# Tile 1 of a fused layer's start in two PSUM buffers, tile 2's statistics later, and other transfer prices in its list scheduler

## The chip, the cores and the metric

One core of one Trainium2 chip runs the whole kernel in one launch. The metric is the device time in microseconds (us), the median of three runs: 467.97 us (467.95 to 468.36) before the change. Beside it stands one profiled execution, of which every instruction is on record.

## The reference

The input x has 2048 rows of 512 numbers, all in float32. It is normalised row by row, goes through a windowed attention and through a two-layer block side by side, and the two results are multiplied:

```python
xn = _layernorm(x)                       # mean and variance over 512, eps 1e-5
qkv = xn @ wqkv                          # 512 x 1536; 32 heads of 16
# attention: position p sees p, p-2, ... p-14 (8 positions), softmax over those
s = attention(q, k, v) @ wo              # 512 x 512
h = relu(xn @ w1 + b1) ** 2              # 512 x 1792
g = silu(h @ w2 + b2)                    # 1792 x 512
out = x + s * g
```

## The kernel before

**Precision and tiles.** A float32 number is split into a high part (`high`, a ScalarE copy to the fast matmul type) and a low part (`low`, a subtraction on VectorE or on an engine that the scheduler chooses); `split` does both. A product of two split operands is three matmuls, high x high, high x low and low x high (`PASSES`, line 48). The rows of x come in 16 tiles of 128 rows. An even tile's split, transposed rows lie in `XA`; those of an odd tile lie half in `odd` and half in `XB`.

**Stages.** First the 16 tiles are normalised, transposed and multiplied with wqkv; the results go from the buffers `stg` to DRAM (`sq`, `sk`, `sv`). VectorE does the attention in eight units on data loaded from there, during most of the rest. Then TensorE does xn @ w1 (`ups`, in products called uX, uY and uZ), then h @ w2 (`down`, pb) mixed with the attention's output product (`out_product`, pw). From tile 4 on some products are made with seven multiplications in place of eight blocks, from sums of operands (`Sf`, `SA`, `SB`).

**Who sets the order.** Every instruction is recorded in a `Book`. A first pass, the draft, records the program; `arrange` (line 428) then plays it through up to 120 times with a list scheduler, `forward` (line 221), which holds a price for every instruction (`price`), a lag per engine (`LAGS`), and one wire for all transfers. It keeps the order whose end was earliest by those prices, and the second pass writes the instructions of each engine in that order. `tails` (line 365) gives each instruction its urgency with the same prices, and `landed` (line 390) adds waits of one DMA issue on an earlier transfer's landing where the plan has it so. TensorE's operations are chained as recorded (in `add`, line 154); the four other queues, SP's DMA issues among them, are the scheduler's to order. A DMA is priced in `add` at 600 ns of issue; in `forward` it takes the wire for its bytes divided by `RATE` (250 bytes per ns), no earlier than 800 ns after its issue, and has landed 1100 ns later.

**The start.** Up to `book.first = False` (line 1044) every queue keeps the order in which the code is written. There stand, for tiles 0 to 2 and the wqkv weights:

- `stats(t)` (line 821): two VectorE instructions for mean and variance (`st`, `mv`), one that adds the epsilon (`rs`), and the step on GpSimd that raises `rs` to the power -0.5 (the power step).
- `norm(t)`: one VectorE instruction that writes the normalised tile `early`; for tile 0 it is cut into two halves.
- `trans(t)` (line 880): four transposes on TensorE into one PSUM buffer `pxT` (`psT`, line 526, two buffers), then the `high` copies. Tile 0 uses both buffers.
- `keep_full(t)`: a ScalarE copy of the transposed tile to `fulls`; `lowx(t)`: the low parts.
- `qkv(t, s)` (line 972): the 12 matmuls of tile t with the q (s = 0), k (s = 1) or v (s = 2) weights, and the copy to `stg`. `late=True` does the products of the tile's high part first.
- The product of tile 0 with the k weights is done in plain float32 (eight instructions of TensorE, `pq<-wqraw,fulls`), with tile 1's transposes ahead of its last two.

The part that the change edits reads, from line 1014:

```python
    stats(1)
    low(*wq_parts(1, 0), V)
    ...
    norm(1)
    ...
    lows(0, 0)
    stats(2)
    qkv(1, 1, None, True)
    lows(0, 2)
    norm(2)
    stats(3)
    book.first = False
    constants()
    qkv(0, 0, lambda: highs(2, 0))
    trans(2)
```

Of the kernel before, what the change touches and what calls it, by code (L numbers as in the profile page):

```python
# [17 lines left out]
P = 128  # L18
# [40 lines left out]
WARM = 20  # L59
WARM2 = 1  # L60

RATE, AHEAD, ROUNDS, SPARE = 250.0, 2500.0, 120, 4000.0

LAGS = dict(P=250, V=160, A=170, G=150)

# [14 lines left out]
def elements(ap):  # L80
    n = 1
    for d in ap.shape[1:]:
        n *= d
    return n


class Book:
# [66 lines left out]
    def add(self, key, name, f, a, k):  # L154
        n = len(self.ops)
        engine = key
        if key == "E":
            engine = self.plan[1][n] if self.plan else "V"
            f = getattr(f[engine], name)
        ins = f(*a, **k)  # L160
        out = k["out"] if "out" in k else a[0]
        outs = [out] + ([k["accum_out"]] if "accum_out" in k else [])
        ins_ = [*(a if "out" in k else a[1:]), *(x for i, x in k.items() if i not in ("out", "accum_out"))]
        ins_ = [x for x in ins_ if isinstance(x, bass.AP)]
        two = sum(x.space != bass.MemoryType.PSUM and elements(x) > 1 for x in ins_) > (name != "tensor_scalar")
        if key == "E":
            op = Op(n, "E", ins, {e: self.price(e, name, k, ins_, out) for e in "VG"}, True)
        elif name == "dma_start":
            moved = 4
            for d in out.shape:  # L170
                moved *= d
            op = Op(n, "S", ins, 600, moved=moved)
        else:
            op = Op(n, engine, ins, self.price(engine, name, k, ins_, out),
                    engine == "V" and two or engine == "G" and elements(out) > 1 and name != "memset")
        op.early = self.first
        if self.first:
            if op.engine in self.heads:
                self.heads[op.engine].starts.append(op)
                op.waits += 1  # L180
            self.heads[op.engine] = op
        func = next((x for x in a if isinstance(x, mybir.ActivationFunctionType)), None)
        op.table = func if func in (AF.Exp, AF.Silu) else None
        op.stream = self.in_stream
        self.ops.append(op)
        if engine == "P":
            if "P" in self.last:
                self.edge(self.last["P"], op)
            self.last["P"] = op
        for x, writes in [(x, False) for x in ins_] + [(x, True) for x in outs]:  # L190
            r = self.region(x)
            if r is None:
                continue
            t, p0, p1, m = r
            writes = writes or t.space == "PSUM"
            if t not in op.tiles:
                op.tiles.append(t)
                if not t.users:
                    used = self.firsts.setdefault(t.slot, [])
                    if len(used) >= t.bufs:  # L200
                        t.behind = used[-1]
                    used.append(op)
                if t.behind not in (None, op):
                    t.behind.starts.append(op)
                    op.waits += 1
                t.users.append(op)
            kept = []
            for other, w, q0, q1, k_ in t.log:
                if (w or writes) and other is not op and p0 < q1 and q0 < p1 and m & k_:
                    self.edge(other, op)  # L210
                if not (writes and p0 <= q0 and q1 <= p1 and k_ & ~m == 0):
                    kept.append((other, w, q0, q1, k_))
            kept.append((op, writes, p0, p1, m))
            t.log = kept
        return ins
# [5 lines left out]
    def forward(self, urgency):  # L221
# [53 lines left out]
        while n:  # L275
# [57 lines left out]
                late = max(0.0, at - urgency[op.n])  # L333
            op.end = at + ns + LAGS.get(e, 0)
            if op.moved:
                wire = max(wire, at + ns + 800) + op.moved / RATE
                op.end = wire + 1100
            end = max(end, op.end)
            order.append(op)
            n -= 1  # L340
# [24 lines left out]
    def tails(self, order=None):  # L365

        extra, last = {}, None
        for op in self.ops:
            if op.stream and op.engine == "V":
                if last is not None:  # L370
                    extra[last.n] = op
                last = op
        follow = [list(op.after) + ([extra[op.n]] if op.n in extra else []) for op in self.ops]
        if order is None:
            order = self.ops
        else:
            for t in self.tiles.values():
                if t.prev is not None:
                    for op in t.prev.users:
                        follow[op.n] += t.users  # L380
        tail = [0.0] * len(self.ops)
        for op in reversed(order):
            ns = op.ns[op.given if order is not self.ops else "G"] if op.engine == "E" else op.ns
            cost = ns + (op.moved / RATE + 1900 if op.moved else LAGS.get(op.given, 150))
            tail[op.n] = max([cost + tail[b.n] if b.engine != op.engine or op.engine != "P" else ns + tail[b.n]
                              for b in follow[op.n]] or [cost])
        top = max(tail)
        return [top - t for t in tail]
# [117 lines left out]
def trace(ctx: ExitStack, tc: tile.TileContext, plan, x, wqkv, wo, w1, b1, w2, b2, out):  # L506
# [28 lines left out]
    def high(hi, lo, src):  # L535
        A.activation(hi, src, AF.Copy)

    def low(hi, lo, src, eng):
        eng.tensor_sub(lo, src, hi.bitcast(F32))
# [429 lines left out]
    def new_stg(t, s):  # L969
        stgs[s] = pstg.tile([P, GR, 2, CH], F32, name=f"stg{t}_{s}", tag="stg", bufs=3)  # L970

    def qkv(t, s, between=None, late=False, new=True):

        ps = psA(f"pq{t}_{s}")
        order = [(kt, a, b) for kt in range(KT) for a, b in PASSES]
        if late:
            order.sort(key=lambda o: o[1])
        for n, (kt, a, b) in enumerate(order):
            PE.matmul(ps, x_of(t, a, kt), wq[2 * s + kt // 2](b, kt % 2), start=n == 0, stop=n == 11,
                      skip_group_check=True)  # L980
            if between and n == 5:
                between()
        evacuate(t, s, ps, new)
# [28 lines left out]
        PE.transpose(pT[kt // 2][:, kt * P:(kt + 1) * P], xn[0][:, kt * P:(kt + 1) * P], ident)  # L1012
    idle(WARM2)
    stats(1)
    low(*wq_parts(1, 0), V)

    x0 = fulls[:, 0]
    for kt in (0, 2):
        cols = slice(kt * P, (kt + 2) * P)
        A.activation(x0[:, cols], pT[kt // 2][:, cols], AF.Copy)  # L1020
    norm(1)
    for kt in range(1, KT):
        split(*wq_parts(1, kt), V)
    for part in parts(0, x0):
        high(*part)
    ps = psA("pq0_1")
    for kt in range(KT):
        if kt == KT - 1:
            trans(1)
            keep_full(1, pTs[1])  # L1030
        PE.matmul(ps, x0[:, kt * P:(kt + 1) * P], raws[1, kt], start=kt == 0, stop=kt == KT - 1)
    lowx(1)
    for part in parts(0, x0):
        low(*part, V)
    evacuate(0, 1, ps)
    for kt in (0, 2):
        highs(0, kt)
    lows(0, 0)
    stats(2)
    qkv(1, 1, None, True)  # L1040
    lows(0, 2)
    norm(2)
    stats(3)
    book.first = False
    constants()
    qkv(0, 0, lambda: highs(2, 0))
    trans(2)
    keep_full(2, pTs[2])
    lows(2, 0)
# [512 lines left out]
```

## Time and profile before

| What | Value |
|---|---|
| Median of three runs | 467.97 us (467.95 to 468.36) |
| Profiled execution, its own time | 467.41 us |
| Its span, first to last instruction | 465.6 us (465.63) |
| TensorE busy | 459.5 us, 2037 matmuls and transposes |
| VectorE busy | 405.4 us |
| ScalarE busy | 302.5 us |
| GpSimd busy | 286.2 us |
| Bytes moved by DMA | 87.77 MB |

The times of the profile count from the span's start. Engines are named PE (TensorE's matmuls), PEld (its weight loads), DVE (VectorE), ACT (ScalarE), POOL (GpSimd) and SP (the queue that issues the DMAs). Almost every row carries line 160, since there the `Book` calls the engine; so rows are told apart by tile names, as out<-in. A row in order of time gives start, duration, engine, operation, tiles, shapes and count, and in brackets how long the engine sat idle before it and what ended that. Instructions of an engine that follow on each other are pipelined, so a row of several can overlap with the next.

### The profile page before, as it was taken

The page shows a single profiled execution, that of the slowest core. Times are in us where ns is not written, and L with a number is a line of the kernel's source. Part 1 is how long each engine was busy: PE and PEld are TensorE (multiplying, and loading weights), DVE is VectorE, ACT ScalarE, POOL GpSimd, SP SyncE. Part 2 cuts the span into 40 slices and gives each one's busy share as a digit, 9 for nine tenths or more (in the row PEclk, how much of TensorE's full clock was granted, in tenths as well). Part 3 has the DMA queues.
Part 4 walks back from the last instruction along what each step waited for, and adds up shares of the span by engine and source line. Part 5 has one row for each costly group of instructions (what it writes and reads, how often), then busy time and mean ns, then how long its engine had stood idle before and what let it go on. Part 6 is the DMA issues. An engine that isn't in the chain of part 4 may idle for free.

```text
span 465.6 us, 6191 instructions
## 1 busy us (share of the span) xinstructions
PE 459.5 (99%) x2037; PEld 378.7 (81%) x2037; DVE 405.4 (87%) x341; ACT 302.5 (65%) x569; POOL 286.2 (61%) x297
## 2 busy tenths in 40 slices
PE   8999999999999999999999999999999999999996
PEld 5788888888888888888888888888888888888885
DVE  5987996499999999999999979999999999589413
ACT  5756976974655748477684898687449544963331
POOL 2286343524999889975361699777656656465340
PEclk9999999999999999999999999999999999999999
DMA  8799789979989993962463395878853886260302
GB/s 277 220 237 280 246 226 280 264 169 277 261 227 263 242 289 126 242 176 69 107 184 75 119 236 176 207 226 259 207 139 101 230 199 204 92 178 25 113 1 91
DMA packets 71484, 87.77 MB, mean 188 GB/s; under 512 B 6684, under 2 KB 50972, under 8 KB 71452
## 3 DMA queue, kind: packets, MB, share of 16 engines
q1 hardware_dynamic: 71452, 87.38, 68.2%
q8 instruction: 16, 0.26, 0.2%
q14 instruction: 16, 0.13, 0.1%
HBM read 53.75 MB, written 30.47 MB: 181 GB/s over the span
## 4 chain that ended last, share of the span: by engine, by line
PE 97%; DVE 1%; DMA 1%; ACT 0%; issue 0%; POOL 0%
PE pb L160 33%; PE uX L160 16%; PE pq L160 13%; PE pm L160 12%; PE pw L160 9%; PE uZ L160 8%; PE uY L160 4%; DMA x<-in_A_x 1%; PE pxT L160 0%; DVE st L160 0%; DVE wq L160 0%; DVE z L160 0%; DVE wq0r L160 0%; DVE XA L160 0%; POOL rs L160 0%
## 5 line engine op out<-in xcount | busy, mean ns | idle before, releaser
L160 PE MATMUL pb<-w,h 128*128 128x512 f32 x592 | 149.1, 389 | 0.0
L160 PEld LDWEIGHTS pb<-w,h 128*128 128x128 f32 x592 | 110.9, 188 | 23.4 <-POOL h L160 0.4
L160 DVE TENSOR_TENSOR pr<-k,qp 128x2048 f32<-128x2048 f32 x32 | 72.8, 2274 | 6.5 <-ACT qp L160 4.8
L160 DVE TENSOR_TENSOR pv<-v,Lp 128x2048 f32<-128x2048 f32 x32 | 73.1, 2285 | 0.9
L160 DVE TENSOR_REDUCE v<-pv 128x256 f32<-128x2048 f32 x32 | 72.9, 2278 | 0.6
L160 DVE TENSOR_REDUCE L<-pr 128x128 f32<-128x2048 f32 x32 | 72.8, 2274 | 0.4
L160 POOL TENSOR_TENSOR h<-ut,h 128x512 fp32r<-128x512 f32 x25 | 32.2, 1299 | 37.4 <-ACT ut L160 30.9
L160 PE MATMUL pw<-wot,oT 128*128 128x512 f32 (+1 forms) x204 | 45.5, 376 | 0.0
L160 PEld LDWEIGHTS pw<-wot,oT 128*128 128x128 f32 x204 | 36.8, 188 | 7.1
L160 POOL TENSOR_TENSOR h<-u,h 128x256 fp32r<-128x256 f32 (+1 forms) x30 | 30.3, 1028 | 18.5 <-ACT u L160 14.8
L160 ACT ACTIVATE h<-ut 128x512 fp32r<-128x512 f32 x28 | 16.4, 626 | 27.5 <-PE pb L160 15.6
L160 PE MATMUL pq<-wq,XA 128*128 128x512 f32 x122 | 31.5, 391 | 0.3 <-DVE wq L160 0.3
L160 ACT ACTIVATE ut<-ut 128x512 f32<-128x512 f32 x42 | 24.9, 627 | 8.7 <-DMA ut<-su 6.4
L160 ACT ACTIVATE u<-uX,b1t 128x512 f32<-128x512 f32 x28 | 19.3, 688 | 17.2 <-PE uX L160 16.8
L160 DVE TENSOR_TENSOR z<-z,pw 128x512 f32<-128x512 f32 (+1 forms) x17 | 11.0, 648 | 20.9 <-ACT z L160 10.8
L160 POOL TENSOR_TENSOR oT<-oTf,oT 128x512 fp32r<-128x512 f32 x16 | 25.5, 1598 | 5.2 <-ACT oT L160 5.2
L160 POOL TENSOR_TENSOR u<-u,more 128x512 f32<-128x512 f32 x14 | 18.1, 1297 | 15.4 <-ACT more L160 15.0
L160 PEld LDWEIGHTS pq<-wq,XA 128*128 128x128 f32 x122 | 22.7, 188 | 5.3 <-DVE wq L160 0.7
L160 ACT ACTIVATE u<-u 128x512 f32<-128x512 f32 (+1 forms) x54 | 26.4, 528 | 0.4
L160 ACT ACTIVATE oT<-oTf 128x512 fp32r<-128x512 f32 x16 | 18.2, 1135 | 11.9 <-PE pw L160 10.2
L160 ACT ACTIVATE stg<-pm 128x512 f32<-128x512 f32 x30 | 17.9, 598 | 12.0 <-PE pm L160 10.3
L160 ACT ACTIVATE stg<-pq 128x512 f32<-128x512 f32 x24 | 14.4, 598 | 16.5 <-PE pq L160 13.6
(165 smaller groups left out, 1003.6 us busy)
## 6 DMA issues: line engine op xcount, KB each, us to landing
k<-sk SPq DMA_DIRECT2D x8, 960.0 KB, 7.5
v<-sv SPq DMA_DIRECT2D x8, 960.0 KB, 9.1
su<-u SPq DMA_DIRECT2D x28, 256.0 KB, 3.3
ut<-su SPq DMA_DIRECT2D x28, 256.0 KB, 3.6
x<-in_A_x SPq DMA_DIRECT2D x16, 256.0 KB, 4.2
sk<-stg SPq DMA_DIRECT2D x8, 512.0 KB, 4.9
sq<-stg SPq DMA_DIRECT2D x8, 512.0 KB, 4.4
sv<-stg SPq DMA_DIRECT2D x8, 512.0 KB, 4.1
```

The costliest lines, as they stand in the source:

```text
L160: ins = f(*a, **k)
```

## The change

It does four things. In the start, `low` of the first k weights moves from ahead of `norm(1)` to behind it. Tile 1 is transposed into two PSUM buffers, two transposes each; its high copies, its copies to `fulls` (now two) and its low parts each read one of them. The statistics of tile 2 (`stats(2)`) come behind the third `low` of the q weights in place of the second, the fourth follows them, and `qkv(0, 0)` does all products with the weights' high parts ahead of those with their low parts (`late` is now the place in the tuple by which the order is sorted: 1 the tile's part, 2 the weights'). And the list scheduler prices a transfer in a new way: 480 ns of issue, and a rate by the length of its contiguous pieces, the shorter of its two sides: 245 bytes per ns from 4096 bytes on, 340 from 2048, and 270 below.

```diff
-RATE, AHEAD, ROUNDS, SPARE = 250.0, 2500.0, 120, 4000.0
+AHEAD, ROUNDS, SPARE = 2500.0, 120, 4000.0
+
+ISSUE, BEFORE, BEHIND = 480, 800, 1100
+RATES = (4096, 245.0), (2048, 340.0), (0, 270.0)
...
+def contiguous(ap):
+    dims = list(ap.ap)
+    if ap.space != bass.MemoryType.DRAM:
+        dims = dims[1:]
+    run = 1
+    for step, count in sorted((d for d in dims if d[1] > 1), key=lambda d: d[0]):
+        if step != run:
+            break
+        run *= count
+    return 4 * run
...
-            op = Op(n, "S", ins, 600, moved=moved)
+            whole = min(contiguous(out), contiguous(k["in_"] if "in_" in k else a[1]))
+            op = Op(n, "S", ins, ISSUE, moved=moved / next(r for size, r in RATES if whole >= size))
...
-                wire = max(wire, at + ns + 800) + op.moved / RATE
-                op.end = wire + 1100
+                wire = max(wire, at + ns + BEFORE) + op.moved
+                op.end = wire + BEHIND
...
-            cost = ns + (op.moved / RATE + 1900 if op.moved else LAGS.get(op.given, 150))
+            cost = ns + (op.moved + 1900 if op.moved else LAGS.get(op.given, 150))
...
-    def qkv(t, s, between=None, late=False, new=True):
+    def qkv(t, s, between=None, late=0, new=True):
...
-            order.sort(key=lambda o: o[1])
+            order.sort(key=lambda o: o[late])
...
     stats(1)
-    low(*wq_parts(1, 0), V)
...
     norm(1)
+    low(*wq_parts(1, 0), V)
     for kt in range(1, KT):
         split(*wq_parts(1, kt), V)
     for part in parts(0, x0):
         high(*part)
+    second = []
     ps = psA("pq0_1")
     for kt in range(KT):
         if kt == KT - 1:
-            trans(1)
-            keep_full(1, pTs[1])
+            place(1)
+            pT = [psT(f"pxT1_{i}") for i in (0, 2)]
+            for i in range(KT):
+                PE.transpose(pT[i // 2][:, i * P:(i + 1) * P], xn[1][:, i * P:(i + 1) * P], ident)
+            for (hi, lo, _), t, cols in zip(parts(1, pT[0]), pT, (slice(0, 256), slice(256, 512))):
+                second.append((hi, lo, t[:, cols]))
+                high(*second[-1])
+            for i, t in enumerate(pT):
+                cols = slice(i * 256, i * 256 + 256)
+                A.activation(fulls[:, 1, cols], t[:, cols], AF.Copy)
         PE.matmul(ps, x0[:, kt * P:(kt + 1) * P], raws[1, kt], start=kt == 0, stop=kt == KT - 1)
-    lowx(1)
+    for part in second:
+        low(*part, V)
     for part in parts(0, x0):
         low(*part, V)
     evacuate(0, 1, ps)
     for kt in (0, 2):
         highs(0, kt)
     lows(0, 0)
+    low(*wq_parts(0, 2), V)
     stats(2)
-    qkv(1, 1, None, True)
-    lows(0, 2)
+    qkv(1, 1, None, 1)
+    low(*wq_parts(0, 3), V)
     norm(2)
     stats(3)
     book.first = False
     constants()
-    qkv(0, 0, lambda: highs(2, 0))
+    qkv(0, 0, lambda: highs(2, 0), 2)
     trans(2)
```

## Rows read from the trace of the kernel before

**Rows 1.** The page, part 1: busy time, share of the span, instructions.

```profile
PE 459.5 (99%) x2037; PEld 378.7 (81%) x2037; DVE 405.4 (87%) x341; ACT 302.5 (65%) x569; POOL 286.2 (61%) x297
```

**Rows 2.** The chain that ended last, in order of time: start, duration, what.

```profile
20.50 21.81 PE pq L160 x96
...
50.47 1.36 PE pq L160 x6
...
65.43 1.47 PE pq L160 x6
...
80.50 1.48 PE pq L160 x6
...
265.58 38.25 PE pb L160 x168
```

**Rows 3.** Instructions in order of time, TensorE's matmuls, 5 to 20.6 us.

```profile
5.78 0.76 PE L160 MATMUL pxT<-ident,early 128*128 128x128 f32 x4 [0.17 <-DVE early L160]
...
6.69 2.84 PE L160 MATMUL pq<-wqraw,fulls 128*128 128x512 f32 x6
...
14.55 0.61 PE L160 MATMUL pq<-wq,XA 128*128 128x512 f32 x2
15.43 1.44 PE L160 MATMUL pq<-wq,XA 128*128 128x512 f32 x5 [0.26 <-DVE wq L160]
16.71 0.60 PE L160 MATMUL pxT<-ident,early 128*128 128x128 f32 x4
...
19.90 0.60 PE L160 MATMUL pxT<-ident,early 128*128 128x128 f32 x4
```

**Rows 4.** The same view, VectorE, 3 to 20.6 us.

```profile
5.32 0.74 DVE L160 TENSOR_SCALAR early<-x,mv,rs 128x256 f32<-128x256 f32 x2 [0.68 <-POOL rs L160]
...
7.24 0.69 DVE L160 TENSOR_TENSOR wq<-wqraw,wq 128x512 fp32r<-128x512 f32 x1
8.38 0.55 DVE L160 TENSOR_SCALAR early<-x,mv,rs 128x512 f32<-128x512 f32 x1 [0.45 <-POOL rs L160]
8.84 1.89 DVE L160 TENSOR_TENSOR wq<-wqraw,wq 128x512 fp32r<-128x512 f32 x3
11.19 0.42 DVE L160 TENSOR_TENSOR odd<-pxT,odd 128x256 fp32r<-128x256 f32 x1 [0.46 <-ACT fulls L160]
...
13.67 0.69 DVE L160 BATCH_NORM_STATS2 st<-x 128x6 f32<-128x512 f32 x1
...
14.68 1.29 DVE L160 TENSOR_TENSOR wq<-wqraw,wq 128x512 fp32r<-128x512 f32 x2
15.89 0.54 DVE L160 TENSOR_SCALAR early<-x,mv,rs 128x512 f32<-128x512 f32 x1
...
18.97 0.55 DVE L160 TENSOR_SCALAR early<-x,mv,rs 128x512 f32<-128x512 f32 x1 [0.44 <-POOL rs L160]
```

**Rows 5.** The same view, GpSimd, 4 to 25 us: the power steps of tiles 0 to 2.

```profile
4.72 0.56 POOL L160 TENSOR_TENSOR rs<-rs,mhalf 128x1 f32<-128x1 f32 x1 [2.42 <-DVE rs L160]
7.38 0.96 POOL L160 TENSOR_TENSOR rs<-rs,mhalf 128x1 f32<-128x1 f32 x1 [2.11 <-DVE rs L160]
14.84 0.95 POOL L160 TENSOR_TENSOR rs<-rs,mhalf 128x1 f32<-128x1 f32 x1 [6.50 <-DVE rs L160]
```

**Rows 6.** The same view, ScalarE, 6 to 14 us: readers of the transposed tile 1.

```profile
10.01 0.39 ACT L160 ACTIVATE odd<-pxT 128x256 fp32r<-128x256 f32 x1 [0.42 <-PE pxT L160]
...
10.55 0.60 ACT L160 ACTIVATE fulls<-pxT 128x512 f32<-128x512 f32 x1
```

**Rows 7.** DMA issues (KB each, median us to landing), then two stretches (busy, PEclk, DMA).

```profile
x<-in_A_x SPq DMA_DIRECT2D x16, 256.0 KB, 4.2
...
w1r<-in_B_w SPq DMA_DIRECT2D x14, 256.0 KB, 4.7
...
8.00:14.00 6.00, 6.00 (x25) 4.09 (x24) 5.16 (x10) 5.56 (x12) 0.34 (x1) 1.00 1.05 395
20.50:42.00 21.50, 21.50 (x96) 17.74 (x96) 18.05 (x35) 11.61 (x24) 18.10 (x15) 1.00 0.99 251
```

## The prediction

> **What bounds the kernel now.** I read the page's busy times first: TensorE is busy for 99% of the span, VectorE for 87% [rows 1]. A busy TensorE need not be one at its peak, so the chain of waits in order of time comes next, for its pace. The reader is to see that it is a clock's pace: six matmuls of 128x512 take 1.36 us wherever nothing holds them up, so one takes 0.227 us, and 96 in a row from 20.50 us take 21.81 us, which is 0.03 us over 96 x 0.227. Where TensorE waits, the same six take longer: 1.47 at 65.43 (0.11 lost) and 1.48 at 80.50 (0.12 lost); and the 168 at 265.58 take 38.25 instead of 38.08 (0.17 lost) [rows 2]. So from 20.5 us to the last matmul the kernel loses about 0.4 us in all. The granted clock has nothing to give either: it is 1.00, the level of 2.4 GHz, in the stretch shown [rows 7].
>
> The start is the third view. From 14.55 to 16.71 us TensorE does seven matmuls; at 0.227 they are 1.59 us, so 0.57 us are lost, and the row at 15.43 names the subtraction that makes a low half of the q weights [rows 3]. Elsewhere between 6.69 and 20.5 us it runs through. The work ahead of 6.69 (first tile's load, statistics, transposes) is not touched by the change.
>
> Together 0.57 + 0.11 + 0.12 + 0.17 = 0.97 us. **That is the most that any order of the same matmuls can give back**, 0.21% of the time; 0.2%, 0.94 us, is about what a measurement of this kernel can tell from no change. The sum is made against the profiled execution, 467.41 us (span 465.63 and 1.78 around it); the median of the three runs is 0.56 above it, and I put the sum on the median.
>
> **Part 1: VectorE up to the second tile.** `low` of the first k weights moves behind `norm(1)`; in the whole start no DMA changes its place, and `qkv(1, 1)` keeps its order. Now it runs from 7.24 to 7.93 beside GpSimd's power step, which takes 0.96 us there and 0.56 for the first tile, where VectorE is idle [rows 4, 5]. Alone, the power step would end at 7.38 + 0.56 = 7.94 and `norm(1)` start at 7.98 instead of 8.38. TensorE gains nothing by it: its six float32 matmuls hold it until 9.53 whatever `norm(1)` does, and the second tile's transposes come behind them [rows 3]. Behind `norm(1)` (0.46 from its start to the next operation's) stand four `low` instead of three, 0.60 from start to start ((1.89 - 0.69)/2) [rows 4]: 7.98 + 0.46 + 4 x 0.60 = 10.84.
>
> **Part 2: two PSUM buffers.** Now VectorE waits 0.46 us, to 11.19, for ScalarE's copy of the whole transposed tile [rows 4]; ScalarE reads the tile from 10.01 to 11.16 [rows 6]. In two buffers each half has its own readers: ScalarE can begin two transposes (about 0.22 us) earlier, at 9.79, and does odd, XB, and two half copies at 0.27 from start to start ((10.55 - 10.01)/2), so the first half is free of ScalarE at about 9.79 + 2 x 0.27 + 0.39 = 10.72. VectorE, there at 10.84, finds it free. The copy in two parts costs ScalarE at most 2 x 0.39 - 0.60 = 0.18 us more, less than the 0.22 it starts earlier, so its four `high` of the q weights come no later than now and stay ahead of VectorE. The second tile's low halves thus start 0.35 us earlier, at 10.84 for 11.19. TensorE again gains nothing, it was not waiting for them.
>
> **Part 3: the third tile's statistics.** From 11.19 to the statistics at 13.67 VectorE spends 2.48 us [rows 4]; changed, that ends at 10.84 + 2.48 = 13.32. There one `low` of the q weights now stands first: 13.92. The statistics hold VectorE for 1.01 us (13.67 to 14.68), so the second `low` follows at 14.93 and ends at 15.62, where both had ended at 15.97. The 12 matmuls of `qkv(0, 0)`, now with all eight products of high weights first, start at 13.42 (five before the row at 14.55) and need the last low weight at 13.42 + 11 x 0.227 = 15.92: **the wait at 15.43 is gone**, and they are through at 16.14.
>
> **What is late next** is the third tile. Its transposes follow `qkv(0, 0)` on TensorE in any order of the draft, and need `norm(2)`, which needs the power step. That step starts 0.16 behind the `low` after the statistics (14.84 against 14.68), and beside a `low` it took 0.96 and 0.95 us [rows 4, 5]; so it runs from 15.09 to 16.04, `norm(2)` from 16.08 to 16.62 (0.54), and the transposes start at about 16.69: the first tile's start at 5.78, within 0.1 of the first half of its norm (5.32 and half of 0.74) [rows 3, 4]. Now they start at 16.71 [rows 3]. So the 0.57 us of waiting stays, as 0.55 between 16.14 and 16.69, and only its releaser changes. Queued behind the late `norm(2)` are the statistics and `norm(3)`, 0.19 us later (18.97 becomes 19.16) [rows 4]; its transposes come at 19.90 now [rows 3], and `norm(3)` would end at 19.71, so that cover still holds, with 0.13 to spare. Bounds for the start: from -0.57 (all of the wait goes) to +0.55 (the power step takes 0.96 only from 15.62 on: 16.58, norm to 17.16, transposes 17.23). I take the middle, -0.02, because both rows of the power step beside a `low` agree on 0.95.
>
> **Part 4: prices of transfers.** They cost nothing on the chip; they change the order in which the draft writes VectorE's, ScalarE's, GpSimd's and SP's instructions after the start. TensorE's order is as recorded, since the draft chains its operations. A load of x rows (256 KB, pieces of 2 KB) falls from 0.60 + 0.80 + 1.05 + 1.10 = 3.55 to 0.48 + 0.80 + 0.77 + 1.10 = 3.15 us; it took 4.2. A w1 load (512 B pieces) falls to 3.35; it took 4.7. So the latencies move away from these medians [rows 7], by up to 0.4 us, though the medians hold waiting in the queue, which the draft adds by itself. The rates move towards the trace: 395 GB/s came through in the first loads (2 KB pieces), 251 where the engines were full with mixed sizes [rows 7]. Below, the most to gain is the 0.40 us lost after 20.5; above, each transfer that a product is made to wait for just in time may come 0.4 us late. I take 0, as the old prices were also short of the medians and lost only 0.4 us in 445.
>
> **Sum:** 467.97 - 0.02 + 0 = 467.95 us.
>
> **Rivals.** *A, the third tile is in time.* If the power step isn't held up by the `low` issued at 14.93 it takes 0.56: it ends at 15.65, `norm(2)` at 16.23, transposes at 16.29, 0.42 earlier: 467.55. For it: the first row of [rows 5]. Against: the other two.
>
> *B, slower: transfers priced too cheap.* Place: loads that are needed just in time behind 20.5 us, where DMA is at a share of 0.99 [rows 7], so the turn, x and w1 loads and all that VectorE and GpSimd make of them. Price: 0.4 us for each load on which TensorE ends up waiting; it decides from the third such wait on (1.2 us). With four, 467.95 + 1.6 = 469.55. For it: both medians in [rows 7] stand above the new price, and VectorE, at 87%, has little room to catch up. Against: the same shortfall stood in the old draft at nearly as much, and only three waits of 0.1 to 0.2 us came of it [rows 2].
>
> *C, the power step is blocked outright.* In the trace it ends 0.41 us behind the `low` it runs beside (8.34 against 7.93) [rows 4, 5]. If it did all of its 0.56 behind it, it would end at 15.62 + 0.56 = 16.18 and the transposes come at 16.83: +0.12, 468.09. The Trainium skill, SBUF — State Buffer, section "Who interferes with whom", says so: a VectorE instruction with two SBUF inputs holds GpSimd's reads off until it is through. The trace agrees that it is held up, but not by the full length.
>
> *D, every wait goes*, also those after 20.5: 467.97 - 0.97 = 467.00.
>
> **How the numbers follow.** Forecast 0.57, A 0.15, B 0.14, C 0.10, D 0.04. Faster than 467.03 is D alone, 0.04; slower than 468.91 is B, 0.14; the rest, 0.82, is within 0.2%. The range reaches from 467.2, below A with some of the small waits gone, to 469.0, which takes in C and two waits at B's price (468.75); left out are D and B from three waits on, about 0.18.
>
> **What would show it.** Right: no idle time named by the low q weights around 15.4 us, but one named by `early` ahead of the transposes at about 16.7; the power step of tile 2 at 0.95 us from about 15.1; VectorE without the 0.46 us ahead of the second tile's low half; first product of tile 2 at about 17.05, as now. Wrong: transposes at 16.3 (A) or 16.8 (C), or, after 20.5 us, stretches of six matmuls above 1.36 us that add up to more than 1 us (B). The forecast is wrong as a whole if the time is more than 0.9 us from 467.95.

## The result, and the profile after

The changed kernel is **slower by 0.42%**: its median is 470.27 us over 16 runs (468.00 to 471.85), that of the kernel before 467.92 over 16 runs beside it (467.27 to 470.07), a ratio of 1.0042 with a 95% interval of 1.0027 to 1.0056 (this ratio goes with the means; the medians stand 0.50% apart). The forecast was 467.95, with 469.0 as the upper end: wrong, on the side of rival B.

The spread says more than the median. Of the 16 runs before, 14 lie between 467.27 and 468.36; the 16 after cover almost 4 us, and the shortest, 468.00, is near the time before. That shortest one is the profiled execution (span 466.2 us), so the rows below show the changed kernel when things went well. One run of `price_only` below, 515.23 us at a mean granted clock of 0.85, was a slow one and is left out of its numbers.

The page's busy times of the kernel after, against [rows 1]:

```profile
PE 460.1 (99%) x2037; PEld 379.8 (81%) x2037; DVE 403.0 (86%) x342; ACT 299.6 (64%) x568; POOL 282.2 (61%) x296
```

Nothing is to be seen in them. The start, in order of time: TensorE against [rows 3], VectorE against [rows 4], GpSimd against [rows 5]:

```profile
7.22 2.84 PE L175 MATMUL pq<-wqraw,fulls 128*128 128x512 f32 x6
...
16.21 0.61 PE L175 MATMUL pq<-wq,XA 128*128 128x512 f32 x2
17.21 0.63 PE L175 MATMUL pxT<-ident,early 128*128 128x128 f32 x4 [0.38 <-DVE early L175]
...
20.42 0.60 PE L175 MATMUL pxT<-ident,early 128*128 128x128 f32 x4
...
7.54 0.55 DVE L175 TENSOR_SCALAR early<-x,mv,rs 128x512 f32<-128x512 f32 x1 [0.67 <-POOL rs L175]
...
11.29 0.42 DVE L175 TENSOR_TENSOR odd<-pxT,odd 128x256 fp32r<-128x256 f32 x1 [0.80 <-ACT fulls L175]
...
15.39 0.68 DVE L175 TENSOR_TENSOR wq<-wqraw,wq 128x512 fp32r<-128x512 f32 x1
16.52 0.55 DVE L175 TENSOR_SCALAR early<-x,mv,rs 128x512 f32<-128x512 f32 x1 [0.44 <-POOL rs L175]
...
6.95 0.55 POOL L175 TENSOR_TENSOR rs<-rs,mhalf 128x1 f32<-128x1 f32 x1 [1.86 <-DVE rs L175]
15.56 0.93 POOL L175 TENSOR_TENSOR rs<-rs,mhalf 128x1 f32<-128x1 f32 x1 [8.05 <-DVE rs L175]
```

The wait for the low q weights is gone, and one named by `early` stands ahead of tile 2's transposes. From 16.21 two matmuls at 0.227 us end at 16.66, so that wait is 17.21 - 16.66 = 0.55 us. All of TensorE lies 0.53 us later than before here, since its first product starts at 7.22 for 6.69; that is not the change (last section). It accounts for most of the 0.59 between the two profiled executions, 468.00 and 467.41. Counted from the first product, tile 3's transposes come after 20.42 - 7.22 = 13.20 us, against 19.90 - 6.69 = 13.21 before: the edits of the start neither gain nor lose anything here, so what the changed kernel loses is lost behind the start.

Then the transfers: issues with median us to landing, then stretches of 10 us (PE, PEld, DVE, ACT, POOL busy, granted clock, DMA share, GB/s; a transfer counts in the stretch where it starts, so a share can pass 1), against [rows 7]:

```profile
x<-in_A_x SPq DMA_DIRECT2D x16, 256.0 KB, 5.6
...
w1r<-in_B_w SPq DMA_DIRECT2D x14, 256.0 KB, 5.3
...
20.50:42.00 21.50, 21.50 (x99) 17.84 (x98) 17.80 (x35) 13.02 (x26) 16.21 (x14) 1.00 1.03 271
50.00:60.00 10.00, 10.00 (x46) 8.15 (x45) 8.47 (x13) 8.24 (x20) 2.00 (x3) 1.00 1.07 267
60.00:70.00 10.00, 10.00 (x45) 8.10 (x45) 9.97 (x12) 9.80 (x24) 5.70 (x10) 1.00 1.04 300
70.00:80.00 10.00, 10.00 (x45) 8.28 (x45) 8.60 (x10) 9.18 (x24) 5.04 (x12) 1.00 1.02 254
```

The kernel before had, in the last three of these stretches:

```profile
50.00:60.00 10.00, 10.00 (x46) 8.29 (x45) 8.97 (x13) 9.98 (x24) 4.29 (x8) 1.00 0.70 228
60.00:70.00 10.00, 10.00 (x45) 8.09 (x45) 9.59 (x8) 6.53 (x14) 4.01 (x8) 1.00 0.84 218
70.00:80.00 10.00, 10.00 (x46) 8.29 (x45) 7.50 (x15) 5.97 (x12) 3.90 (x4) 1.00 1.05 267
```

The engines of the DMA had some room from 50 to 70 us before (0.70 and 0.84); after, there is none, and the same loads take longer to land, 5.6 us for 4.2 and 5.3 for 4.7. ScalarE is fuller too from 60 to 80 us: 9.80 and 9.18 us busy for 6.53 and 5.97. With the new prices the plan has transfers go out earlier: SP issues the x rows of tiles 14 and 15 at 64.52 and 65.07 us, for 77.47 and 77.87 before. The work that hangs on such transfers can come earlier with them.

**Where the lost time is** has to be read in a longer execution, not in the shortest. The changed kernel was run again, unaltered (`after_again`).

> The changed kernel once more, for a profile of one of its longer executions (its runs lay between 468.0 and 471.85 us; the first profile was of one of 468.0). Theory P: TensorE's waits behind 20.5 us add up to 1.5 to 3 us more than in the first profile, and follow a transfer's landing. Theory S: the extra time is lost ahead of 20.5 us, in the start or in the level of the clock there.

Median 468.86 over 12 runs (468.15 to 473.45), ratio 1.0037 (1.0016 to 1.0058): the loss and the spread are there again, though the median is 1.4 us below that of the first 16 runs. The profile is of an execution of 470.45 us. What TensorE waited for in it (total us, times, longest):

```profile
PE pq L175 <- ACT stg L175: 1.1, 1, 1.1
PE pxT L175 <- DVE early L175: 0.4, 1, 0.4
```

The second stands in that view of the shortest execution too; the first does not. Counted from start to start of TensorE's matmuls, with 0.227 us taken off each, the execution of 470.45 us loses 2.6 us behind 20.5 us and the shortest 0.3. Of the 2.6, 1.4 are lost at 82.4 us, where this wait is; the rest is in losses of 0.1 to 0.4 us each, the larger ones ahead of matmuls that read `SA` (60.0 us) and `h` (295.6 and 323.2 us). What led to those was not followed. The longest one can be followed back, instruction by instruction (in order of time, VectorE, ScalarE, TensorE, `after_again`):

```profile
74.06 1.32 DVE L175 STREAM_TRANSPOSE pxT<-turn 128x512 f32<-128x512 f32 x2 [1.33 <-DMA turn<-turn]
...
74.83 0.60 ACT L175 ACTIVATE XA<-pxT 128x512 fp32r<-128x512 f32 x1 [1.00 <-DVE pxT L175]
75.42 0.39 ACT L175 ACTIVATE odd<-pxT 128x256 fp32r<-128x256 f32 x1
...
81.27 0.60 ACT L175 ACTIVATE stg<-pm 128x512 f32<-128x512 f32 x1
81.74 0.61 ACT L175 ACTIVATE stg<-pq 128x512 f32<-128x512 f32 x1
...
82.40 0.97 PE L175 MATMUL pq<-wq,odd 128*128 128x512 f32 x3 [1.12 <-ACT stg L175]
```

and the same instructions in the shortest execution of the same kernel:

```profile
72.54 1.31 DVE L175 STREAM_TRANSPOSE pxT<-turn 128x512 f32<-128x512 f32 x2
...
73.53 0.59 ACT L175 ACTIVATE XA<-pxT 128x512 fp32r<-128x512 f32 x1
...
80.32 0.62 ACT L175 ACTIVATE stg<-pq 128x512 f32<-128x512 f32 x1
...
80.99 1.66 PE L175 MATMUL pq<-wq,odd 128*128 128x512 f32 x6
```

The four loads of turned tiles 10 and 11 (`turn`) were issued within 0.2 us of each other in the two (66.52 and 66.70), and the last landed at 72.41 in the one and 73.94 in the other. VectorE's transposes, ScalarE's copy `XA` and the ScalarE copy that empties the PSUM buffer (`stg<-pq`) follow 1.52, 1.30 and 1.42 us later. ScalarE has no gap from 74.83 to 83.05, so it hands on all of its delay, and TensorE starts 1.41 later. In the kernel before, ScalarE reached the same evacuation with three gaps behind its `XA` copy, 1.34 + 0.70 + 1.04 = 3.08 us; by an estimate that takes what ended these gaps as not hanging on the load, a late load could have eaten that much (ScalarE in order of time, before):

```profile
76.23 0.60 ACT L160 ACTIVATE Lp<-L 128x512 f32<-128x512 f32 x1 [1.34 <-POOL L L160]
77.53 0.60 ACT L160 ACTIVATE stg<-pm 128x512 f32<-128x512 f32 x1 [0.70 <-DMA sv<-stg]
79.18 0.60 ACT L160 ACTIVATE stg<-pm 128x512 f32<-128x512 f32 x1 [1.04 <-PE pm L160]
```

### The profile page after: what moved, and what is told of

Its sections match the earlier page's. It is cut to its first block, busy times and chain, and to the rows that moved or that the text cites. A ratio compares the mean times of both kernels' runs of the same rounds, so it can differ in the third digit from the quotient of the medians.

```text
span 466.2 us, 6205 instructions
## 1 busy us (share of the span) xinstructions
PE 460.1 (99%) x2037; PEld 379.8 (81%) x2037; DVE 403.0 (86%) x342; ACT 299.6 (64%) x568; POOL 282.2 (61%) x296
## 4 chain that ended last, share of the span: by engine, by line
PE 97%; DVE 1%; POOL 0%; issue 0%; ACT 0%; DVEq 0%; POOLq 0%
PE pb L175 33%; PE uX L175 16%; PE pq L175 13%; PE pm L175 12%; PE pw L175 9%; PE uZ L175 8%; PE uY L175 4%; PE warm L175 1%; PE pxT L175 0%; DVE wq L175 0%; POOL rs L175 0%; DVE z L175 0%; DVE wq0r L175 0%; DVE st L175 0%; DVE XA L175 0%
## 5 line engine op out<-in xcount | busy, mean ns | idle before, releaser
L175 POOL TENSOR_TENSOR h<-ut,h 128x512 fp32r<-128x512 f32 x23 | 29.6, 1294 | 40.7 <-ACT ut L175 36.3
L175 POOL TENSOR_TENSOR h<-u,h 128x256 fp32r<-128x256 f32 (+1 forms) x32 | 32.0, 1022 | 21.1 <-ACT u L175 20.0
```

## The experiments

**1. The two halves of the change, apart.** `start_only` is the changed kernel with the old prices, `price_only` the kernel before with the new ones.

```diff
 # start_only, against the kernel after
-AHEAD, ROUNDS, SPARE = 2500.0, 120, 4000.0
...
-ISSUE, BEFORE, BEHIND = 480, 800, 1100
-RATES = (4096, 245.0), (2048, 340.0), (0, 270.0)
+RATE, AHEAD, ROUNDS, SPARE = 250.0, 2500.0, 120, 4000.0
...
-            op = Op(n, "S", ins, ISSUE, moved=moved / next(r for size, r in RATES if whole >= size))
+            op = Op(n, "S", ins, 600, moved=moved)
...
```

> The edits of the start alone, with the old transfer prices. Theory P (the new prices make a plan in which transfers are needed just in time, and their varying landing turns into waits of TensorE): 467.9 us, within 0.2% of the kernel before, with its spread of about 1 us. Theory S (the start itself got worse): about 470 us, and the profile shows over 1.5 us more lost on TensorE ahead of 20.5 us than the kernel before. Theory R (any new order that the scheduler draws has its own tight places, whatever edit caused it): anything from 467 to 471 us, the loss in the profile lying behind 20.5 us.

> The new transfer prices alone, with the old start. Theory P: 469.5 to 470.5 us with a spread of 2 us or more, as the changed kernel, and the loss is behind 20.5 us. Theory S: 467.9 us. Theory R: anything from 467 to 471 us, and not the same waits as in the changed kernel.

`start_only`: 468.88 us (468.64 to 469.24, 9 runs), ratio 1.0024 (1.0015 to 1.0033). `price_only`: 470.19 us (469.51 to 470.28, 5 runs), ratio 1.0044 (1.0031 to 1.0057). So each half costs time alone, and the prices cost more than twice as much. No theory met both: P had said 467.9 for `start_only`, and for `price_only` a spread of 2 us or more. Neither has a wide spread (0.6 and 0.8 us), so the spread of the changed kernel is not brought about by the new prices as such.

The loss of `start_only` is in the start (TensorE, VectorE and GpSimd in order of time, `start_only`):

```profile
17.08 0.63 PE L160 MATMUL pxT<-ident,early 128*128 128x128 f32 x4 [0.58 <-DVE early L160]
...
19.46 1.50 DVE L160 TENSOR_SCALAR early<-x,mv,rs 128x512 f32<-128x512 f32 x1 [0.44 <-POOL rs L160]
...
19.40 1.28 POOL L160 TENSOR_TENSOR wq<-wqraw,wq 128x512 fp32r<-128x512 f32 x1
```

`norm(3)` takes 1.50 us in place of 0.55, beside a subtraction on GpSimd that began 0.06 us ahead of it, and tile 3's transposes come 0.82 us late; ahead of tile 2's, TensorE loses 0.85 us, for 0.55 in the kernel after. With the old prices the draft gives that subtraction to GpSimd at that point; with the new ones it does not (after, `norm(3)` takes 0.55 and nothing waits for it). So this cost belongs to a draft, not to the edits of the start as such.

The profile of `price_only` shows three waits of TensorE for `stg`, at 65.7, 81.6 and 97.9 us; the second is at the place of the wait of `after_again` (total us, times, longest):

```profile
PE pq L175 <- ACT stg L175: 2.0, 3, 1.1
```

That is its loss, but its own plan had waits of 1.28 us at 81.0, 0.58 at 96.6 and 0.30 at 111.9, 2.2 us in all, since the draft played by the new prices did not find a better order. So `price_only` does not tell a bad plan from a plan that is missed. The next runs do.

**2. The rates alone.** The changed kernel, with the old 600 ns for an issue.

```diff
-ISSUE, BEFORE, BEHIND = 480, 800, 1100
+ISSUE, BEFORE, BEHIND = 600, 800, 1100
```

> The changed kernel with the rates by length of pieces but the old 600 ns of issue. Theory T1 (the rates are what is too cheap): transfers behind 50 us land later than the plan has it, as in the changed kernel by 1 to 3 us, and runs spread over 2 us or more, median 469 to 470.5. Theory T2 (the issue price is what is too cheap): landings at or ahead of the plan, spread under 1 us, median 468 to 468.9.

470.79 us (470.19 to 471.59, 5 runs), ratio 1.0060 (1.0046 to 1.0073). Theory T2 is out, and T1 missed its figures: the median is above its band, and the spread is 1.4 us. This plan has no waits of its own behind the start and still loses 2.8 us. Behind 20.5 us the profiled execution, of 470.31 us, loses 2.3 us, ahead of matmuls that read the `SA` sums, at 74.2 (0.25) and 75.5 (0.34), and `h`, at 349.2 (0.34) and 393.5 (0.65), with about 0.1 behind each (what TensorE waited for, total us, times, longest, `rates_only`):

```profile
PE pb L175 <- POOL h L175: 0.7, 2, 0.5
PE pm L175 <- POOL SA L175: 0.2, 1, 0.2
```

The rates suffice for a loss; the price of an issue is not needed: `start_only`, which differs from this run in the rates alone, took 468.88 us. The waits are at other places than in `after_again`, so it is no single load that was misplaced. That these waits follow from a late landing is not shown.

**3. Plan against trace.** Each draft leaves a planned landing for each transfer, and the traces have the real ones. The table takes the transfers issued from 40 to 125 us and gives the median of real less planned landing; then how far TensorE itself stands behind its plan there, on average; the difference is how early (below 0) the data came for those who wait for it. The runs are the profiled executions.

```
                landing - plan   TensorE - plan   difference
before              -2.13           -0.4            -1.7
start_only          -0.31           +1.0            -1.3
stats_first         +0.22           +1.7            -1.5
price_only          +0.99           +0.9            +0.1
after               +1.03           +1.1            -0.1
after_again         +1.67           +1.9            -0.2
rates_only          +0.82           +1.3            -0.5
```

With the old prices the data came 1.3 to 1.7 us ahead of plan, with the new ones between 0.5 us ahead and on plan. Nobody had written a margin into the old prices; most of it goes with the flat rate of 250, for `start_only`, which has that rate, stands at -1.3 and `rates_only`, which differs from it in the rates alone, at -0.5. In the kernel before, 1.3 of its 1.7 us are there at the issue already: the transfers go out that much ahead of plan, by the same reckoning. On plan in the median means late for nearly half of the transfers, and in the kernel after a tenth of them came 1.1 us late or more.

**4. The x rows ahead of a late load, moved behind it.** The changed kernel's plan is kept, instruction by instruction, but SP issues the turned tiles 10 and 11 ahead of the x rows of tiles 14 and 15, which stood before them.

```diff
-        plan = trace(draft_tc, None, *copies)
-    trace(tc, plan, *aps)
+        order, given, landed = trace(draft_tc, None, *copies)
+    loads, rows = (545, 546), (541, 542, 543, 544)
+    order = [n for n in order if n not in loads]
+    at = max(order.index(n) for n in rows) + 1
+    order[at:at] = loads
+    landed = [(n, m) for n, m in landed if not (n in loads or n in rows and m in loads)]
+    trace(tc, (order, given, landed), *aps)
```

> The changed kernel with its own plan kept to the letter, but for one thing: the two loads of x rows (tiles 14 and 15, 512 KB) that SP issues just ahead of the four transfers that turn tiles 10 and 11 are issued just behind those. Theory T (a full DMA queue makes the turned tiles land late; VectorE's transposes of them wait, ScalarE's copies of those wait with the evacuations queued behind them, no PSUM buffer comes free, TensorE waits at about 81 us): the turned tiles land 1.5 to 2 us earlier, no execution waits at 81 us, the runs above 469.5 us become rare, median 468.3 to 468.9. Theory U (the executions differ for another reason, such as the clock or the end): same median and spread as the changed kernel, 468 to 473 us.

474.59 us (472.55 to 477.49, 6 runs), ratio 1.0146 (1.0114 to 1.0178): far slower, and the expectation missed. The turned tiles were issued no earlier: the first of the four went out at 66.52 us, as in the shortest execution of the kernel after (66.52) and 0.18 us before that of `after_again`, though two loads fewer stood ahead of it. The last of them landed at 72.15, for 72.41 and 73.94. But the plan lets the next issue, a load of k, wait for the landing of the x rows, so that it went out at 73.14 in place of 69.74, the store of `stg` behind it landed at 81.53 for 78.10, and the buffer was free that much later (ScalarE and TensorE in order of time, then windows with the granted clock as the third number from the end, `moved`):

```profile
81.61 0.60 ACT L175 ACTIVATE stg<-pm 128x512 f32<-128x512 f32 x1 [2.85 <-DMA sv<-stg]
...
84.67 2.93 PE L175 MATMUL pq<-wq,odd 128*128 128x512 f32 x6 [3.59 <-ACT stg L175]
...
84.00:85.00 1.00, 0.33 (x1) 0.33 (x2) 1.00 (x2) 0.98 (x2) 0.09 (x1) 0.50 1.03 269
...
90.00:91.00 1.00, 1.00 (x6) 0.83 (x5) 0.25 (x1) 0.88 (x2) 0.00 (x0) 1.00 1.09 129
```

The move was no test of the one load, since it came no earlier on SP. It does show the mechanism a second time, by another transfer: a landing, then ScalarE in order, then the PSUM buffer, then TensorE. And it shows how little slack is around: two issues exchanged with four cost 4 us and more. Part of that is the clock: behind the pause of 3.59 us TensorE ran at a granted clock of 0.50 (last section).

**5. The start, another way.** The start of the changed kernel at the old prices, but with the statistics of tile 2 ahead of both `low`.

```diff
-    low(*wq_parts(0, 2), V)
     stats(2)
     qkv(1, 1, None, 1)
-    low(*wq_parts(0, 3), V)
+    lows(0, 2)
```

> Old prices; of the start's edits all but the last: the third tile's statistics stay ahead of both remaining low parts of the q weights. By the theory of the start (the low part that is issued between the statistics and the norm holds the power step up, and the transposes of the third tile wait for it) the power step ends about 0.6 us earlier than with the start's edits alone, and the wait ahead of the third tile's transposes (0.85 us there) falls under 0.3 us, with at most 0.2 us come back ahead of the products with the low q weights. The rival (the wait follows from the two PSUM buffers and the later first low part) leaves it at 0.8 us. Time 468.0 to 468.6 against 468.9 of the start's edits alone, if the new plan has no waits of its own.

470.02 us (469.41 to 470.49, 5 runs), ratio 1.0043 (1.0029 to 1.0056): the expectation missed, with a wait of 1.00 us where under 0.3 was said. GpSimd, VectorE and TensorE in order of time, `stats_first`:

```profile
16.54 1.35 POOL L160 TENSOR_TENSOR wq<-wqraw,wq 128x512 fp32r<-128x512 f32 x1
...
16.68 1.49 DVE L160 TENSOR_SCALAR early<-x,mv,rs 128x512 f32<-128x512 f32 x1
...
18.32 0.63 PE L160 MATMUL pxT<-ident,early 128*128 128x128 f32 x4 [1.00 <-DVE early L160]
```

The draft put a subtraction of GpSimd beside `norm(2)` this time, with the price seen in `start_only`: 1.49 us for 0.55. The power step began at 15.62, no earlier than in the kernel after, as the draft had also slipped another VectorE instruction ahead of the statistics. So it says nothing of where the statistics are best placed; it repeats the blocked norm. Behind 23 us this execution has one wait, for `stg` at 127.7 us (0.5 us), and its own plan has one there too. With the old prices, then, neither `start_only` nor `stats_first` shows a wait behind 23 us that its plan lacks; the three plans drawn with the new prices all do (1.3 us at 82.4 in `after_again`, four of 0.25 to 0.65 in `rates_only`, 0.46 at 65.7 in `price_only`). The plan of the kernel before shows none in its own profile, and one of 0.3 us, at 321.5, in `late_frozen` (experiment 7). So three plans on each side speak against any new order having such tight places of its own (Theory R), but do not rule it out.

**6. Margin, tested directly.** If the margin in the plan is what counts, the same extra load must cost the kernel after, and not the kernel before. Both plans are kept as they are; on the chip the stores of two transposed tiles (6 and 7) write each row twice, 512 KB more, into a spare place of which half is read back. The output's computation is unchanged.

```diff
-        dma(sr[t], full)
+        if plan and t in (6, 7):
+            dma(wide[t - 6], full[:, None, :].to_broadcast([P, 2, D]))
+        else:
+            dma(sr[t], full)
...
-            dma(raw[t][i], sr[t][:, i * 256:(i + 1) * 256])
+            src = wide[t - 6][:, 0] if plan and t in (6, 7) else sr[t]
+            dma(raw[t][i], src[:, i * 256:(i + 1) * 256])
```

> The kernel before with its own plan, in which the two stores of transposed tiles 6 and 7 write twice the bytes (each row also into a spare place that nobody reads): 512 KB more, about 2 us of the DMA engines, at 53 to 67 us. Theory M (the old prices left transfers landing ahead of the plan by more than 1 us, and that margin hides a disturbance): the time stays within 0.5 us of the kernel before, and no wait over 0.5 us appears on TensorE between 55 and 125 us. Rival N (both plans are as tight, and the changed one only met worse luck): 1 to 2 us slower, with such a wait.

> The same added 512 KB in the changed kernel with its own plan, at about 63 us. Theory M (the new prices left no margin): 2 us or more slower than the changed kernel (470 us and more at the least, median 471.5 to 474), with a wait of 2 us or more on TensorE at 81 us behind evacuations of ScalarE. Rival N: slower by as much as the kernel before is with the same bytes.

`before_2x`: 467.94 us (467.26 to 468.42, 11 runs), ratio 0.9997 (0.9988 to 1.0005). `after_2x`: 470.88 us (469.83 to 471.33, 6 runs), ratio to the kernel before 1.0060 (1.0048 to 1.0072); its shortest run is 1.8 us above the shortest of the kernel after, its median a little under the band expected. Against the kernel after, which was not run beside it, the median is 0.6 us higher (first 16 runs) or 2.0 (`after_again`), and 15 of those 28 runs are shorter than its shortest; Theory M had said 2 us or more. TensorE at the critical place in `before_2x`:

```profile
80.18 1.64 PE L160 MATMUL pq<-wq,odd 128*128 128x512 f32 x6
```

and the chain in `after_2x` (VectorE, ScalarE, TensorE in order of time):

```profile
75.16 1.32 DVE L175 STREAM_TRANSPOSE pxT<-turn 128x512 f32<-128x512 f32 x2 [1.99 <-DMA turn<-turn]
...
82.83 0.60 ACT L175 ACTIVATE stg<-pq 128x512 f32<-128x512 f32 x1
...
83.48 1.65 PE L175 MATMUL pq<-wq,odd 128*128 128x512 f32 x6 [1.71 <-ACT stg L175]
```

The same bytes cost nothing in the old plan. In the new one the wait of `after_again` is 1.71 us for 1.12, by the same chain, 1.1 us later at each link; a wait of 2 us or more had been expected. The transfers that land just before the added bytes go out are 0.1 to 0.2 us later than in `after_again`, the last turned tile 1.1 us. Where the bytes went in the old plan is seen at the DMA engines (windows as above, first `before_2x`, then `after_2x`):

```profile
60.00:70.00 10.00, 10.00 (x46) 8.09 (x45) 9.59 (x8) 6.53 (x15) 3.99 (x8) 1.00 0.91 241
...
60.00:70.00 10.00, 9.83 (x43) 7.71 (x42) 10.00 (x12) 9.89 (x25) 5.50 (x10) 1.00 1.05 318
```

The share rises from 0.84 to 0.91, and the x and w1 loads land after 4.2 and 4.5 us (medians), no later than without the bytes (4.2 and 4.7): the engines had room, so little of the data's lead over the plan was used up. By their times and profiles, then, the old plan has room for this disturbance and the new one has not; what the bytes cost in the new one is not settled. The pair does not tell apart the three kinds of room that the old plan has: on the DMA engines, in the landings, and in ScalarE's gaps.

**7. One edit of the start, in the old plan.** The plan of the kernel before is kept, and only the 12 matmuls of `qkv(0, 0)` change their order: high weights first, as in the change.

```diff
-    qkv(0, 0, lambda: highs(2, 0))
+    qkv(0, 0, lambda: highs(2, 0), 2 if plan else 0)
```

(`qkv` takes `late` as the place to sort by here too, as in the change.)

> The kernel before with its own plan kept, in which only the order of the 12 matmuls of tile 0 with the q weights is changed to high weights first. By the prediction's reading of the start (TensorE waits 0.57 us for the last low q weights, and the third tile's norm is through at 16.44): the wait falls to 0.1 to 0.3 us, the transposes of the third tile start at about 16.5, and the time is 0.2 to 0.45 us below the kernel before, 467.5 to 467.75, less than a measurement can tell. Rival (the wait moves whole to the transposes, whose norm is the later one in any order): 467.9, no wait named by the q weights, one of over 0.4 us named by the norm.

467.86 us (467.18 to 468.62, 11 runs), ratio 0.9996 (0.9987 to 1.0004): no difference that shows. The wait for the low q weights shrinks to 0.13 us, and 0.32 us of waiting comes up ahead of tile 2's transposes, so 0.45 of the 0.57 stays, most of it under another name, as the prediction had it for the whole change. Both forecasts had part of it: the wait for the weights fell as the first one said, and the norm took over most of what was won, as the rival said. With Part 3 thus at nothing and the prices at a loss, no version here is clearly faster than the kernel before.

## Why the prediction was wrong, point by point

**What bounds it, and the most to be won**: held. No run came out clearly below the kernel before.

**Part 1**: the power step alone was put at 0.56 us and took 0.55. `norm(1)` was put at 7.98 and came at 7.54: the power step began at 6.95 for 7.38, because tile 1's statistics started at 5.78 for 6.21: tile 0's norm came 0.19 us earlier in this execution, and the short wait for x that they had before was not there. TensorE gained nothing by it, as said.

**Part 2**: 10.84 was said for the second tile's low halves, 11.29 measured; less the 0.53 by which TensorE was late, 10.76. VectorE was there early and waited 0.80 us for ScalarE, where the prediction had said that it would find the half free; nobody waited for VectorE. That wait belongs to the late start: in `after_2x`, where the start is the same code and the first product comes at 6.55 us, VectorE does the low half at 10.62 without one:

```profile
10.62 0.42 DVE L175 TENSOR_TENSOR odd<-pxT,odd 128x256 fp32r<-128x256 f32 x1
```

**Part 3**: right in what happened and in size. The wait for the low weights went; the wait ahead of the transposes was said to be 0.55 us, named by `early`, and is 0.55 (0.52 in `after_2x`, so the agreement to the hundredth is luck); the power step was put at 0.95 and took 0.93. Rival A (a step of 0.56) and rival C are out: the step ended at 16.49, 0.42 us behind the `low` that ended at 16.07, not 0.56. What Part 3 missed shows only at the old prices: the cover of `norm(3)`, put at 0.13 us to spare, fails if the draft puts a GpSimd subtraction beside it (`start_only`). The step reckoned with GpSimd being held up by VectorE, not with the reverse.

**Part 4** is the step that failed: "I take 0, as the old prices were also short of the medians and lost only 0.4 us in 445." The term put at 0 measured +2.35 us between the medians of the 16 runs and +0.9 in `after_again`; the start added nothing to it. That the old prices lost only 0.4 us is true, but not a reason for 0. The price of one load without a queue (3.55 us old, 3.15 new) was set against a median that contains the queue (4.2 us), and so the old prices looked short. With the queue that the draft adds, they were not short: by the plan of before, the landings stood 1.7 us later than they came. The text noted that the draft adds the queue by itself, and that the new rates move towards the trace, but drew the wrong sign from it: with rates nearer to the trace the margin went. That could have been seen beforehand, by laying the plan of the kernel before beside its trace.

**Rival B** had the place and the mechanism, loads that are needed just in time behind 20.5 us, and its 469.55 is, of all the forecasts, the nearest to 470.27. Its price was wrong: 0.4 us a wait, from the difference of two prices, where single waits took 1.1 and 1.7 us. In the one that was followed back, what set its size is not the price but how much the landing differed between two executions (1.5 us for the turned tiles) less what slack ScalarE had left. And its "against" (the same shortfall stood in the old draft) was the same mistake as in Part 4, so the 0.14 rested in part on a wrong reason. That its 469.55, four waits at 0.4 us, lies between the two medians of the changed kernel, 468.86 and 470.27, is luck.

**Left open.** What makes the same loads land 1.5 us apart in two executions was not found; the issues were within 0.2 us. The two traces agree on every recorded landing from 20 to 59 us to within 0.23 us; then the landings part, by 0.7 us at an x load that lands at 60.2 us in the one and 60.9 in the other, and by 0.9 to 1.5 us at the four turned tiles. Why the changed kernel spreads over 4 us and more, and `price_only` and `rates_only` do not, is open. The issue price of 480 ns was not run by itself. The 2.2 us that `price_only` loses are about what its own plan has in waits, so it is little evidence for missed landings; of its waits only the one at 65.7 us (0.46) is not in its plan.

## What to carry to other kernels

Here a planner whose transfers land on plan in the median had no margin, and nearly half of them came late: before "correcting" a price that seems too high, compare planned with real landings, and keep what the spread between executions needs. When a change leaves the shortest run where it was and widens the spread, look at one of the longer runs, and follow its waits back to the first landing. The carrier to look for is an engine without gaps in its own order; here ScalarE, which empties the PSUM buffers, passed on 1.4 of 1.5 us in the one wait that was followed.

## What the runs showed of the hardware

**A normalisation held up by GpSimd.** VectorE's `norm` (a tensor_scalar, 128x512, float32) took 0.55 us alone and 1.50 and 1.49 us beside a GpSimd subtraction that began 0.06 and 0.14 us earlier (1.28 and 1.35 us long). It ended 0.28 us behind GpSimd both times (20.96 against 20.68, 18.17 against 17.89). The Trainium skill, SBUF — State Buffer, section "Who interferes with whom", says that a tensor_scalar can, in a mode that uses two ports, take the pair of ports that the two engines share, and that whoever issues first holds it for its whole instruction while the other stands still. The traces agree on who waits; the 0.28 us left afterwards are about half of the norm's 0.55.

**The clock after a long wait.** In `moved`, TensorE stood idle for 3.59 us ahead of 84.67, and the granted clock was then 0.50, the level of 1.2 GHz, until 89.9 us (0.57 in the stretch from 89 to 90 us); six matmuls took 2.93 us where they take 1.65 elsewhere. In no profile with waits of up to 1.7 us behind the start was that seen.

**A start that varies by half a microsecond.** The first float32 product began at 7.22 us in the profile of the kernel after, and at 7.22 also in that of `late_frozen`, whose start up to there is that of the kernel before, where it began at 6.69. Tile 0's four transposes tell the two apart, 1.06 us long in the late ones (here `late_frozen`) and 0.76 in [rows 3]:

```profile
6.12 1.06 PE L160 MATMUL pxT<-ident,early 128*128 128x128 f32 x4
...
7.22 1.02 PE L160 MATMUL pq<-wqraw,fulls 128*128 128x512 f32 x1
```

What differs is TensorE's clock. The twenty transposes that it does first, on nothing but the identity, take 3.81 us in the kernel before and 4.53 in `late_frozen`:

```profile
1.80 3.81 PE L160 MATMUL warm<-ident 128*128 128x128 f32 x20 [1.80 <-POOL ident masks.py:199]
...
1.80 4.53 PE L160 MATMUL warm<-ident 128*128 128x128 f32 x20 [1.80 <-POOL ident masks.py:199]
```

In the kernel before they follow each other every 0.213 us up to 4.63 us and every 0.109 us from 4.79 us on; in the kernel after and in `late_frozen` all twenty, and tile 0's four, are 0.213 us apart. The trace's record of the granted clock has its first entry, 1.00, at 4.73 us in the kernel before, at 7.19 in the kernel after and at 7.91 in `late_frozen`; nothing is recorded ahead of it. So the engine does the same work from 1.80 us on, close to half as fast at first, as between the two levels of 1.2 and 2.4 GHz, and the rise comes up to 3.2 us apart in these three executions.

A single profile of either kernel can thus be 0.5 us off in its start alone, which is more than the whole change of the start was worth.
